# An adaLN block with an S4D convolution and a feed-forward: in block 0, the low part of the first layer's weights by an adding transfer instead of a VectorE subtraction

## The chip, the cores and the metric

The program runs on one core of a Trainium2 chip. The metric is the device time of one execution in microseconds (us). The times given are medians of several runs of the same program.

## The reference

One sequence of 2048 tokens, D = 576 channels, feed-forward width 4608, all in fp32:

```python
mod = (_silu(c) @ w_mod).reshape(c.shape[0], 6, 1, -1)
sa, ca, ga, sb, cb, gb = (mod[:, 0], ..., mod[:, 5])
h = _layernorm(x) * (1 + ca) + sa
x = x + ga * S4D(h)
h = _layernorm(x) * (1 + cb) + sb
x = x + gb * (jnp.maximum(h @ w1, 0) @ w2)
```

`S4D(h)` is a long convolution of each channel with a kernel K that is summed from 128 complex exponentials (`P = jnp.exp((A * dt[:, None])[:, :, None] * pos)`, `K = 2.0 * jnp.einsum("dn,dnl->dl", C, P).real`), plus a skip term.

## The kernel before, in words

**Blocks and chunks.** The tokens are cut into NB = 4 blocks of 512, the hidden channels into NF = 36 chunks of 128. `ffn` (L1242) is one loop over g = 0 to 143, that is block by block and in each block over the 36 chunks. Beside it, in its `step` (L1345), it advances generators that hold all other work: while block 0's feed-forward runs, the rest of the convolution kernel is built and block 1's convolution is done; while block 1's runs, block 2's convolution, and so on.

**Two pieces of each number.** TensorE (PE) multiplies in a format (`fp32r`) that keeps fewer bits than fp32. So every weight and activation is split into a high piece, the rounded value, and a low piece, the remainder, and products of high and low pieces are added up. For the first layer `first(g)` (L1296) issues 14 matmuls of 128x512 into a PSUM tile `hps`, from the weights' pieces `w[:, 0]` (high) and `w[:, 1]` (low) and the block's activations `xh`, `xl`, `xs`. ScalarE (ACT) then takes `hh` = Relu of it (L1314), and VectorE (DVE) the remainder `hl` (L1315). `second(g)` (L1318) issues 14 matmuls from `hh`, `hl` and the second layer's pieces into five accumulators `acc` (L1335).

**The weights' path in block 0.** For each chunk `load_r1` (L1254) brings 320 KB of w1 into a tile `r1` (two buffers), `load_r2` (L1258) 288 KB of w2 into `r2` (two buffers), both on SyncE's (SP's) queue. `hi1` (L1274) is an ACT copy of `r1` into `w1[:, 0]`, which rounds to the high piece. `lo1` (L1279) is a DVE subtraction that writes `r1 − high` to `w1[:, 1]`. `hi2` and `lo2` (L1284, L1290, L1291) do the same for the second layer. The low pieces are then stored to DRAM (`L1d`, `L2d`, L1390, on SP's queue, by way of the list `late`), and blocks 1 to 3 load them from there (`low1`, L1263) instead of making them again; so `lo1` computes only for g < 36. The tiles `w1` and `w2` have three buffers each. A buffer of `r1` comes free for chunk g + 2 when `hi1(g)` and `lo1(g)` have read it.

The loop's order for each g is: `load_r1(g+3)`, `load_r2(g+2)`, the stores in `late`, `first(g)`, `hi2` and `lo2` of g + 1, `hi1` and `lo1` of g + 2, `low1(g+3)`, then `second(g−1)`. Instructions of g < 3 are kept in program order (the profile shows them at the helper's line, L47). For the others a list scheduler decides the order on each engine at build time; at run time each engine and each issuing queue goes through its own list in order and waits where an operand isn't ready.

**The other work of block 0.** `rest` (L436) builds the convolution kernel in 12 heads (h = 0 to 11). For each head POOL's queue loads `W0` (768 KB from `W1d`), `Zr` (96 KB from `Zd`) and `W2r` (1536 KB from `W2d`); DVE turns `W0` into `W1r` by rotations (L464 to L470); PE multiplies `W1r` by `W2r` into `kps` (L498); ACT copies that into `ker` (L508), which is stored as `kd` on SP's queue. A load of `W2r` waits until PE is through with the tile's last use, and everything behind it on POOL's queue waits with it. Then follows block 1's convolution: POOL's queue loads `kt` from `kd` (L1232), PE transforms it into `ps_f` (L829), ACT copies that (L830), DVE does butterflies and complex products with spectra `R`, `Ka`, `Ua` that POOL's queue saves to and loads from DRAM (L816, L820). The inverse goes through `ps_i` (L1036). At the end of block 0 the generator is run out, so that block 1's activations are ready.

The functions and what calls them:

Of the kernel before, what the change touches and what calls it, by code (L numbers as in the profile page):

```python
# [10 lines left out]
F32 = mybir.dt.float32  # L11
F32R = mybir.dt.float32r
I32 = mybir.dt.int32
AF = mybir.ActivationFunctionType
ALU = mybir.AluOpType
# [9 lines left out]
NF = F // P  # L25
# [525 lines left out]
class Body:  # L551
# [194 lines left out]
    def main(self, ctx, kg, hooks):  # L746
# [32 lines left out]
        with ExitStack() as c:  # L779
            self.cps = self.pool(c, "cps0", space=PSUM)  # L780
            self.tps = self.pool(c, "tps", space=PSUM)
            self.cv = self.pool(c, "cv0", side="right")
            self.cvl = self.pool(c, "cvl", side="right")
            self.nps, self.ns = 4, 6
            mods, ffn = self.mod_late(), self.ffn(gens)
            self.vec = Kept(tc, nc.vector)
            for w in self.conv(0):
                if w == "mod":
                    next(mods, None)
                elif w in ("weights", "high", "low"):  # L790
                    next(ffn)
                elif w == "rows":
                    hooks[w]()
                elif w in hooks:
                    for _ in hooks[w]:
                        pass
            self.vec = nc.vector
# [444 lines left out]
    def ffn(self, gens):  # L1242

        nc, I, ff = self.nc, self.I, self.ff
        n = NB * NF
        r1, r2, w1, w2 = {}, {}, {}, {}
# [20 lines left out]
        def vec(g):  # L1267
            return (Kept(self.tc, nc.vector) if g < 3 else nc.vector).tensor_tensor

        def copy(g):  # L1270
            return (Kept(self.tc, nc.scalar) if g < 3 else nc.scalar).activation

        def hi1(g):
            copy(g - 1)(w1[g][:, 0], r1[g], AF.Copy)  # L1274

        def lo1(g):
            w, r = w1[g], r1.pop(g)
            if g < NF:
                vec(g)(w[:, 1], r, w[:, 0], op=ALU.subtract)  # L1279
                late.append((self.L1d[g], w[:, 1].rearrange("p k c -> p (k c)")))  # L1280

        def hi2(g):
# [89 lines left out]
        for f in (hi1, hi2):  # L1372
            f(0)
        hi1(1)
        yield
        lo1(0)
        lo2(0)
        lo1(1)
        yield
        load_r2(1)  # L1380
        load_r1(2)
        prev = None
        for g in range(n + 1):
            if g < n:
                if g + 3 < n:
                    load_r1(g + 3)
                if g + 2 < n:
                    load_r2(g + 2)
                for dst, src in late:
                    nc.sync.dma_start(out=dst, in_=src.bitcast(F32))  # L1390
                late.clear()
                new = (g, *first(g))
                if g + 1 < n:
                    hi2(g + 1)
                    lo2(g + 1)
                if g + 2 < n:
                    hi1(g + 2)
                    lo1(g + 2)
                if g + 3 < n:
                    low1(g + 3)  # L1400
                step(g)
            if prev is not None:
                second(*prev)
                if prev[0] % NF == NF - 1:
                    self.evacuate(prev[0] // NF)
            if g < n:
                prev = new
                step(g)
                if g % NF == NF - 1:
                    for _ in gens[g // NF]:  # L1410
                        pass
                    done[0] = 0.0
# [126 lines left out]
```

## Time and profile before

| | us |
|---|---|
| median of 3 runs | 1362.46 (1361.05 to 1364.14) |
| profiled execution | 1357.89 |
| its span | 1356.1 |

The mean granted clock of TensorE was 0.944 of full speed in the profiled execution. The stages on its time axis are: kernel rows and block 0's convolution until about 222 us, block 0's feed-forward from 222 to about 570 us, of which the heads take 222 to 425 and block 1's convolution 425 to 545, and then blocks 1 to 3 until 1356.

How to read it: PE is TensorE's matmuls, PEld its weight loads, DVE VectorE, ACT ScalarE, POOL GpSimd, SPq the queue of SyncE. A row of a timeline gives start, duration, engine, line, operation and in square brackets the idle time before it and what ended that. A wait row reads "engine, tile and line, waited for what: us in total, times, longest". L12 is line 12 of the kernel; `out<-in` names tiles.

### The profile page before, as it was taken

Reading aid. Unit: us, or ns where it says so; the run is one execution under the profiler, and the core shown is the slowest. Engines: PE = TensorE matmul, PEld = TensorE weight load, DVE = VectorE, ACT = ScalarE, POOL = GpSimd, SP = SyncE. Lnnn points to the kernel's source line nnn. Section 1 sums busy time; section 2 is a strip of 40 time slices with the busy share of each in tenths; the row PEclk is TensorE's granted clock in tenths of the full one; section 3 lists DMA queues with packets and bytes.
Section 4 is the critical chain, followed back from the end, with each engine's and each line's share of the span. In section 5 each row is a group of like instructions: output and inputs, shape, how many; then the busy total and the mean of one; then the engine's idle time right before and its main releaser. Section 6 shows DMA issues by size and latency. Waiting matters only on the chain.

```text
span 1356.1 us, 26019 instructions
## 1 busy us (share of the span) xinstructions
PE 1239.6 (91%) x10720; PEld 986.5 (73%) x10720; DVE 891.6 (66%) x1324; ACT 494.9 (36%) x863; POOL 162.6 (12%) x260
## 2 busy tenths in 40 slices
PE   4566777899989999999999999999999999999997
PEld 2345555677767687777777887887888888888885
DVE  5889988999955899678556986367997222111112
ACT  5678423222122432622234225433322353233231
POOL 0657511000010100020000000100000000000000
PEclk9558887999978999999999999999999999999998
DMA  8557973776897877798778995777996557666651
GB/s 267 221 223 291 328 271 130 282 249 248 320 332 277 296 248 269 239 382 311 250 246 327 363 371 158 269 230 245 370 387 194 176 175 228 201 195 195 201 184 53
DMA packets 120843, 345.85 MB, mean 255 GB/s; under 512 B 23916, under 2 KB 24212, under 8 KB 109972
## 3 DMA queue, kind: packets, MB, share of 16 engines
q1 hardware_dynamic: 103828, 226.96, 49.7%
q0 software_dynamic: 16384, 115.85, 22.8%
q8 instruction: 84, 1.38, 0.4%
q10 hardware_dynamic: 512, 1.38, 0.3%
q14 instruction: 35, 0.29, 0.1%
HBM read 262.73 MB, written 81.40 MB: 254 GB/s over the span
## 4 chain that ended last, share of the span: by engine, by line
PE 73%; DVE 15%; DMA 5%; issue 4%; ACT 1%; POOL 1%; SPq 0%; ACTq 0%; DVEq 0%; POOLq 0%
PE acc L1335 29%; PE hps L1309 29%; PE kps L498 4%; PE ps_f L829 4%; PE kps L71 2%; PE ph L71 2%; PE ps_i L1036 2%; DVE T L464 1%; DVE W1r L466 1%; DVE T L62 1%; DMA Ua<-Ud 1%; DVE Y L1015 1%; DMA r<-in_w_dram 1%; DMA kd<-ker 1%; DVE W L62 1%
## 5 line engine op out<-in xcount | busy, mean ns | idle before, releaser
L1309 PE MATMUL hps<-xh,w 128*128 128x512 f32 x1152 | 391.3, 400 | 0.7 <-ACT xh L47 0.7
L1335 PE MATMUL acc<-w,hh 128*128 128x512 f32 x1152 | 371.8, 403 | 7.0 <-ACT hh L1314 7.0
L1315 DVE SCALAR_TENSOR_TENSOR hl<-hps,hh 128x512 fp32r<-128x512 f32 x144 | 99.0, 687 | 322.9 <-ACT hh L1314 321.9
L1335 PEld LDWEIGHTS acc<-w,hh 128*128 128x128 f32 x1152 | 217.6, 190 | 55.1 <-ACT hh L1314 8.3
L1309 PEld LDWEIGHTS hps<-xh,w 128*128 128x128 f32 x1152 | 217.3, 190 | 48.5 <-ACT xh L47 1.3
L1309 PE MATMUL hps<-xl,w 128*128 128x512 f32 x576 | 230.7, 401 | 0.2
L1335 PE MATMUL acc<-w,hl 128*128 128x512 f32 x576 | 224.4, 402 | 3.9 <-DVE hl L1315 3.9
L1314 ACT ACTIVATE hh<-hps 128x512 fp32r<-128x512 f32 x144 | 85.9, 597 | 304.0 <-PE hps L1309 302.3
L1284 ACT ACTIVATE w<-r 128x576 fp32r<-128x576 f32 x141 | 96.6, 685 | 236.7 <-PE acc L1335 207.9
L1335 PEld LDWEIGHTS acc<-w,hl 128*128 128x128 f32 x576 | 109.1, 190 | 28.2 <-DVE hl L1315 5.0
L1309 PEld LDWEIGHTS hps<-xl,w 128*128 128x128 f32 x576 | 108.7, 189 | 24.5 <-DVE xl L47 0.8
L1274 ACT ACTIVATE w<-r 128x640 fp32r<-128x640 f32 x140 | 102.6, 733 | 40.6 <-DMA r<-in_w_dram 40.6
L1309 PE MATMUL hps<-xs,w 128*128 128x512 f32 x288 | 97.1, 410 | 0.3 <-DVE w L1279 0.3
L498 PEld LDWEIGHTS kps<-W1r,W2r 128*32 128x32 f32 x3456 | 66.9, 146 | 32.0 <-issue 23.6
L498 PE MATMUL kps<-W1r,W2r 128*32 128x48 f32 (+2 forms) x3456 | 75.9, 238 | 9.2 <-issue 8.2
L71 PE MATMUL kps<-W,W 128*32 128x16 f32 x2304 | 45.1, 218 | 42.7 <-POOL W L68 28.7
L71 PEld LDWEIGHTS kps<-W,W 128*32 128x32 f32 x2304 | 40.4, 150 | 55.0 <-POOL W L68 30.7
L1015 DVE TENSOR_TENSOR Y<-Y,T 128x1152 f32<-128x1152 f32 x60 | 79.4, 1349 | 0.0
L830 ACT ACTIVATE Z<-ps_f 128x288 f32<-128x288 f32 x120 | 48.7, 408 | 68.8 <-PE ps_f L829 67.6
L1453 POOL DMA_DIRECT2D out_dram<-x x16 | 8.7, 544 | 469.0 <-DVE x L1445 466.3
L1309 PEld LDWEIGHTS hps<-xs,w 128*128 128x128 f32 x288 | 53.3, 188 | 12.4 <-DVE w L1279 0.7
L1335 PE MATMUL acc<-hl,w 128*128 128x512 f32 x144 | 57.3, 398 | 0.0
(230 smaller groups left out, 1567.3 us busy)
## 6 DMA issues: line engine op xcount, KB each, us to landing
r<-in_w_dram SPq DMA_DIRECT2D x144, 320.0 KB, 3.5
r<-in_w_dram SPq DMA_DIRECT2D x144, 288.0 KB, 3.7
w<-L1d SPq DMA_DIRECT2D x108, 320.0 KB
w<-L2d SPq DMA_DIRECT2D x108, 288.0 KB, 2.6
W2r<-W2d POOLq DMA_DIRECT2D x18, 1536.0 KB, 8.3
W2d<-W SPq DMA_DIRECT2D x12, 1536.0 KB, 8.6
Ua<-Ud POOLq DMA_DIRECT2D x15, 1152.0 KB, 9.4
W<-W1d POOLq DMA_DIRECT2D x18, 768.0 KB, 10.7
```

The costliest lines, as they stand in the source:

```text
L62: self.tc.keep_in_program_order(self.nc.vector.tensor_tensor(out, a, b, op=op))
L71: self.tc.keep_in_program_order(self.nc.tensor.matmul(*args, **kw))
L498: nc.tensor.matmul(ps[32 * dd : 32 * dd + 32, q, :], W2[:, r, :, ch], W1[:, :, r, ch], start=(r == 0), stop=(r == 1),)
L829: nc.tensor.matmul(o, fc[:, n2, c, :], src(n2), start=True, stop=True)
L830: ev = nc.scalar.activation(Z[:, n2, c], ps[:, :PC], AF.Copy)
L1015: v(y, y, T, op=op or ALU.add)
L1274: copy(g - 1)(w1[g][:, 0], r1[g], AF.Copy)
L1284: copy(g)(w[:, 0:D], r2[g], AF.Copy)
L1309: nc.tensor.matmul(ps, a, x, start=(i == 0), stop=(i == 13))
L1314: nc.scalar.activation(hh, ps, AF.Relu)
L1315: nc.vector.scalar_tensor_tensor(hl, ps, 0.0, hh, op0=ALU.max, op1=ALU.subtract)
L1335: nc.tensor.matmul(acc[i], a, x, start=(f == 0 and seen[i] == 1), stop=(f == NF - 1 and seen[i] == (3 if i < 4 else 2)),)
```

## The change

In block 0 (g < 36) the DVE subtraction of `lo1` goes. ACT makes a second copy of `r1`, scaled by −1, into `w1[:, 1]`: the negated high piece. Then a transfer on POOL's (GpSimd's) queue reads `r1` and adds it to what stands in `w1[:, 1]`, which leaves `r1 − high`. The store to `L1d` and the next load into the same `r1` buffer wait for this transfer where they waited for DVE. The second layer's low piece stays a DVE subtraction. There are 36 such copies and 36 such transfers of 320 KB. From here on the changed kernel's lines are numbered five higher (Relu L1319, `acc` L1340, `hi2` L1289, the stores L1395).

```diff
         def hi1(g):
             copy(g - 1)(w1[g][:, 0], r1[g], AF.Copy)
+            if g < NF:
+                copy(g - 1)(w1[g][:, 1], r1[g], AF.Copy, scale=-1.0)
 
         def lo1(g):
             w, r = w1[g], r1.pop(g)
             if g < NF:
-                vec(g)(w[:, 1], r, w[:, 0], op=ALU.subtract)
+                nc.gpsimd.dma_start(
+                    out=w[:, 1].rearrange("p k c -> p (k c)").bitcast(F32),
+                    in_=r.rearrange("p k c -> p (k c)"), accum_op=ALU.add,
+                )
                 late.append((self.L1d[g], w[:, 1].rearrange("p k c -> p (k c)")))
```

The scheduler also moves other instructions. Three places follow. The first is POOL's queue at the start of block 0's feed-forward, where the first heads' data are loaded. Before:

```order
L47 DMA W2r_0_2963<-W2d_0_65 128x3072
L47 DMA W0_1_2965<-W1d_1_78 128x1536
L47 DMA Zr_1_2966<-Zd_1_90 128x192
L47 DMA W0_2_2987<-W1d_2_79 128x1536
L47 DMA Zr_2_2988<-Zd_2_91 128x192
L47 DMA W2r_1_3072<-W2d_1_66 128x3072
```

and with the change, where `w1_2666` and `w1_2989` are chunks 2 and 3:

```order
L47 DMA W2r_0_2965<-W2d_0_65 128x3072
L47 DMA W0_1_2967<-W1d_1_78 128x1536
L47 DMA Zr_1_2968<-Zd_1_90 128x192
L1281 DMA w1_2666<-r1_2938 128x640
L47 DMA W0_2_2990<-W1d_2_79 128x1536
L47 DMA Zr_2_2991<-Zd_2_91 128x192
L1281 DMA w1_2989<-r1_2940 128x640
L47 DMA W2r_1_3076<-W2d_1_66 128x3072
```

Chunk 2's adding transfer stands behind the loads of `W2r_0` and `W0_1`, and two adding transfers stand ahead of `W2r_1`.

The second place is POOL's queue at the end of the heads. Before, the last `W2r`, block 1's `x` and the convolution's `kt` follow one another; with the change, where `w1_4898`, `w1_5102` and `w1_5251` are chunks 19, 20 and 21:

```order
L47 DMA W2r_10_4777<-W2d_10_75 128x3072
L47 DMA W2r_11_4924<-W2d_11_76 128x3072
L1281 DMA w1_4898<-r1_4839 128x640
L47 DMA x2_1_5201<-in_x_dram 128x2304
L1281 DMA w1_5102<-r1_5019 128x640
L1281 DMA w1_5251<-r1_5205 128x640
L1232 DMA kt_5203<-kd_1_0_59 128x16x72
```

`kt` now stands behind three adding transfers. In the same way the loads of `Ua` and `R` of the second half of block 1's convolution stand behind the transfers of chunks 26 to 29.

The third place is ACT's list there. Before, `w1_5230` is chunk 21, and its copy stands ahead of the last four copies of kernel heads:

```order
L1314 ACTIVATE hh_5220<-hps_5191 128x512
L1274 ACTIVATE w1_5230<-r1_5185 128x640
L508 ACTIVATE ker_6_4333<-kps_4916 128x16x6
L508 ACTIVATE ker_6_4333<-kps_4975 128x16x6
L508 ACTIVATE ker_6_4333<-kps_5040 128x16x6
L508 ACTIVATE ker_6_4333<-kps_5108 128x16x6
L1284 ACTIVATE w2_5316<-r2_5187 128x576
L1314 ACTIVATE hh_5312<-hps_5275 128x512
```

With the change, chunk 21 is `w1_5251`:

```order
L1319 ACTIVATE hh_5240<-hps_5211 128x512
L508 ACTIVATE ker_6_4349<-kps_4935 128x16x6
L508 ACTIVATE ker_6_4349<-kps_4994 128x16x6
L508 ACTIVATE ker_6_4349<-kps_5059 128x16x6
L508 ACTIVATE ker_6_4349<-kps_5128 128x16x6
L1289 ACTIVATE w2_5337<-r2_5207 128x576
L1274 ACTIVATE w1_5251<-r1_5205 128x640
L1276 ACTIVATE w1_5251<-r1_5205 128x640
L1319 ACTIVATE hh_5333<-hps_5296 128x512
```

Both copies of chunk 21 (L1274, and L1276 negated) now stand behind the heads' copies and the second layer's copy, just ahead of the next Relu.

## The prediction

> **What bounds the kernel now.** I read the page's first rows, then busy time by stretch, then what TensorE (PE) waits for, then the chain of waits. In the windows the columns are the stretch and its length in us, busy us with instruction counts of PE, PEld, DVE, ACT and POOL, the granted clock, the DMA share and GB/s.
>
> ```profile
> span 1356.1 us, 26019 instructions
> ...
> PE 1239.6 (91%) x10720; PEld 986.5 (73%) x10720; DVE 891.6 (66%) x1324; ACT 494.9 (36%) x863; POOL 162.6 (12%) x260
> ```
> ```profile
> 222.00:253.00 31.00, 26.57 (x115) 19.94 (x118) 29.64 (x34) 11.03 (x18) 4.22 (x8) 0.94 0.71 274
> 253.00:350.00 97.00, 93.86 (x1240) 73.77 (x1232) 97.00 (x101) 22.89 (x40) 7.95 (x15) 0.97 0.73 259
> 350.00:425.00 75.00, 65.95 (x1488) 53.35 (x1488) 45.28 (x62) 14.54 (x31) 8.03 (x14) 0.86 0.87 312
> 425.00:525.00 100.00, 100.00 (x421) 76.59 (x420) 88.71 (x136) 34.63 (x70) 7.56 (x13) 1.00 0.81 287
> 525.00:545.00 20.00, 17.12 (x73) 13.07 (x71) 19.78 (x27) 5.61 (x9) 0.00 (x0) 1.00 0.46 165
> 840.00:1120.00 280.00, 280.00 (x1240) 227.02 (x1239) 172.40 (x242) 109.45 (x196) 12.35 (x22) 1.00 0.73 253
> ```
>
> Block 0's feed-forward runs from 222 to about 570. From 253 to 350, while kernel heads are built, VectorE (DVE) is busy for all of 97.0 us; from 525 to 545 for 19.78 of 20. From 425 to 525 PE is full, and later blocks look like 840 to 1120: PE full, and without this subtraction. So time won or lost in block 0 is carried to the end, and the prize is what PE idles in block 0. Its waits, in us, times and longest, from 222 to 253, 253 to 350, 350 to 425 and 425 to 570:
>
> ```profile
> PE acc L1335 <- ACT hh L1314: 3.8, 2, 2.8
> ...
> PE acc L1335 <- ACT hh L1314: 3.1, 1, 3.1
> ...
> PE kps L498 <- issue: 8.2, 3, 2.8
> PE kps L498 <- ACT ker L508: 0.9, 1, 0.9
> ...
> PE acc L1335 <- DVE hl L1315: 1.7, 1, 1.7
> PE ps_i L1036 <- DVE x L1041: 0.9, 1, 0.9
> PE hps L1309 <- DVE w L1279: 0.3, 1, 0.3
> ```
>
> The 9.1 us at the heads' end (8.2 + 0.9) have no cause in the subtractions. That leaves 3.8 + 3.1 + 2.9 = 9.8 us. The chain (start, duration, what) shows the heads' two paces:
>
> ```profile
> 251.93 3.34 DVE W1r L466 x2
> ...
> 271.29 3.34 DVE W1r L466 x2
> ...
> 280.17 11.73 DMA r<-in_w_dram
> ...
> 307.55 2.95 PE hps L1309 x13
> ...
> 326.11 2.95 PE hps L1309 x13
> ```
>
> While DVE leads, a head (two chunks) takes 271.29 − 251.93 = 19.36 us; once a late w1 load has let PE fall behind, PE leads at 326.11 − 307.55 = 18.56.
>
> **The change part by part.** The groups: VectorE's and ScalarE's (xcount, busy us, mean ns), then DMA from 222 to 570 (queue: packets, MB, share of 16 engines; issues with KB and median us to landing).
>
> ```profile
> L1279 DVE TENSOR_TENSOR w<-r,w 128x640 fp32r<-128x640 f32 x33 | 26.8, 816 | 0.0
> ...
> L1274 ACT ACTIVATE w<-r 128x640 fp32r<-128x640 f32 x35 | 25.7, 733 | 37.2 <-DMA r<-in_w_dram 37.1
> ...
> q1 hardware_dynamic: 21952, 48.44, 39.6%
> ...
> W2r<-W2d POOLq DMA_DIRECT2D x12, 1536.0 KB, 8.3
> r<-in_w_dram SPq DMA_DIRECT2D x37, 320.0 KB, 5.2
> ```
>
> *Removed: the subtraction.* 33 × 0.816 = 26.8 us of DVE in these 348 us. Those under the convolution before 222 lie beside other waits; I price them at nothing, and at no more than their own 3 × 0.82 = 2.5 us if that cover is gone. In the heads, two fewer per head give DVE 19.36 − 1.63 = 17.73 us, under PE's 18.56. PE then sets the pace from the start: 97 us are five heads, 5 × 18.56 = 92.8, a gain of 4.2. I take **−4** (ends 0 and −4.2). What is late next is PE itself.
>
> *Added: the negative copy on ScalarE (ACT).* 36 × 0.733 = 26.4 us. ACT is busy 22.89 of 97, 14.54 of 75 and 34.63 of 100 us, so idle time covers it; behind each copy in ACT's order stands often the next Relu (hh), and one copy ahead of it costs PE 0.73 us where hh is awaited. Three such waits stand above, so 0 to 2.2; I take 0, as the Relu has a chunk's time of slack elsewhere.
>
> *Added: the adding transfer.* No row shows one. Below: a plain 320 KB transfer. At q1's rate, 39.6% of 348 us for 48.44 MB, 0.328 MB take 0.93 us of all 16 engines. Above: two such, 1.86 us, as for a load and a store. At one per 10.5 us (348 / 33) the share rises by 0.09 to 0.18: to 0.82–0.91 in the heads, 0.96–1.05 from 350 to 425, 0.90–0.99 from 425 to 525. Only the middle stretch can overflow, by at most 0.05 × 75 = 4 us, and there the heads' last loads go. I take **+1** (0 to +4), nearer the lower row since the 75 us hold some loads with slack.
>
> The Trainium skill, Collectives: The Full Stack, section "The bandwidth ceiling: the fold count and why AG ≠ RS ≠ AR", says an add in the DMA path reads two sources and ran at 1/1.93 of a copy's rate; by it, an estimate, a transfer takes 0.93 × 1.93 = 1.8 us and the term would be about +3. No run here shows it yet.
>
> *Moved: what stands behind it on POOL's queue, and the loads that it frees.* POOL issues in order. At the start the third chunk's transfer comes behind W2r and W0, and the wait of the next w1 load, formerly for DVE, is for its landing:
>
> ```profile
> 227.43 0.53 POOL L47 DMA_DIRECT2D W2r<-W2d  x1 [9.53 <-PE hps L1309]
> ...
> 230.92 0.33 SPq L1254 DMA_DIRECT2D r<-in_w_dram  x1
> ...
> 240.32 0.74 ACT L1274 ACTIVATE w<-r 128x640 fp32r<-128x640 f32 x1 [7.23 <-DMA r<-in_w_dram]
> ...
> 239.82 0.82 DVE L47 TENSOR_TENSOR w<-r,w 128x64 fp32r<-128x64 f32 x2
> ...
> 240.70 0.33 SPq L1258 DMA_DIRECT2D r<-in_w_dram  x1
> ...
> 250.13 0.68 ACT L1284 ACTIVATE w<-r 128x576 fp32r<-128x576 f32 x1 [8.01 <-DMA r<-in_w_dram]
> ```
>
> W2r at 227.43 + 8.3 lands near 236, the transfer near 238, so the load goes at 238 instead of 230.92; in a less crowded queue it takes 5.2, not 9.4, and lands near 243, some 3 us later than 240.3. The wait of 8.01 ends with an r2 load, issued at 240.70 once DVE had made the second layer's low part at 239.82, which the change leaves there. It sets when PE goes on after 250, so 3 us lost at the first place shorten PE's 2.8 us at the second by as much. I take **0** (−1.5 to +4).
>
> From 350 on, chunk 21's transfer stands ahead of the convolution's kt load, and chunk 29's ahead of the next Ua and R loads:
>
> ```profile
> 404.54 1.18 POOL L1232 DMA_DIRECT2D kt<-kd  x1
> ...
> 423.37 0.68 ACT L1284 ACTIVATE w<-r 128x576 fp32r<-128x576 f32 x1 [0.17 <-PE acc L1335]
> ...
> 434.31 0.65 PE L829 MATMUL ps_f<-kt,fcK 128*128 128x288 f32 x2
> ```
> ```profile
> kt<-kd POOLq DMA_DIRECT2D x2, 576.0 KB, 11.8
> ```
>
> kt was issued 30 us before PE used it. Now hi1(21) and its negative copy follow the ACT copy at 423.37, so POOL gets to kt at about 423.37 + 0.68 + 2 × 0.73 + 0.5 = 426; with the median 11.8 us it lands at 438, 3.5 us late, while with W2r's 8.3 it comes in time. PE's order puts the feed-forward's matmuls behind ps_f, so lateness is paid. I take **+2** (0 to +4).
>
> *The tail.* From 525 to 545 the DVE chain sets the end; two subtractions lie in it, and the 425 to 525 stretch drops some ten:
>
> ```profile
> 525.22 1.36 DVE L1013 TENSOR_TENSOR T<-Ka,Ua 128x1152 f32<-128x1152 f32 x1 [2.03 <-DMA Ua<-Ud]
> ...
> 528.50 0.82 DVE L1279 TENSOR_TENSOR w<-r,w 128x640 fp32r<-128x640 f32 x1
> ...
> 538.19 0.82 DVE L1279 TENSOR_TENSOR w<-r,w 128x640 fp32r<-128x640 f32 x1
> ```
>
> That would win back PE's 2.9 us, but DVE already waits 2.03 us there for Ua, which comes no earlier. I take **−2.5** (−2.9 to +2, if Ua or R come later by as much as that wait).
>
> **Sum.** −4 + 0 + 0 + 1 + 0 + 2 − 2.5 = −3.5 us. The profiled execution took 1357.89 us (1356.1 plus 1.8 around it), so 1354.4 like for like; the median of the runs, 1362.46, lies 4.6 above it, so the median becomes **1359.0**. The likeliest case's own range is 1355 to 1361.
>
> **Rivals.** *Transfers come late and the two r1 buffers decide (slower).* A buffer's turn is the load (5.2), two copies (1.5), the adding transfer, and some 2 us of issue. Two buffers pace a chunk at (8.7 + L)/2 us, which exceeds the present 10.5 once the landing L passes 12.3. An adding transfer behind W2r takes 8.3 + 5.2 = 13.5, and others 5.2: mean 9.4, not enough. If its own part doubles, as two passes would, the mean is (18.7 + 10.4)/2 = 14.6, the pace 11.6, and over the 19 chunks until the heads end (203 us / 10.5) it costs 19 × 1.1 = 21 us, with no gain: about 1383; half as often behind W2r, about 1373. For it speak the wait of 7.23 and the 11.73 us load in the chain, with DMA share 0.73 to 0.87; against it that PE needs only one chunk per 9.3 us and waits for w1 loads now in few places.
>
> *Queues eat the gain (slower).* All upper ends of POOL's moved transfers come together, start +4, kt +4, middle +4, tail 0, against −4 in the heads: +8, with half of it +4: 1366 to 1370. It speaks for this that kt loses nearly all its 30 us of lead, and that the Trainium skill, DMA: Bandwidth & Descriptors, section "Issuing engines are not separate DMA queues", has all issuers share the 16 engines; the shares here, 0.87 for both queues together, agree.
>
> *No change.* DVE was never what PE lacked: in the heads only one wait of 3.1 us is booked to a hh, behind a w1 load, not to DVE. Then the heads give −1 at most, the tail −1, kt +2: 1362.5. Against it stands DVE's 97.0 of 97.
>
> **How the numbers follow.** My sum 0.42; queues eat the gain 0.23; buffers decide 0.17; no change 0.18. About 0.2% (2.7 us) is what a measurement of this kernel can tell. Faster 0.40 (the sum's case less its slow edge), same 0.18, slower 0.42: the two slower cases together outweigh the likeliest one, which gives the time. The range leaves out a better heads stage (below 1353) and the worst of the buffers (above 1379): 1353 to 1379.
>
> **What would show it.** Right: PE's busy share from 253 to 350 rises to the full stretch and the heads end some 4 us earlier; DVE shows idle time there; PE's wait at 242 grows and that at 252 shrinks; L1281 lands within 10 us of its issue. Wrong: PE waits for hh behind w1 loads (ACT w ← DMA r grows past 37.1 us), ps_f waits for kt by more than 4 us, or hps waits for w's low part, which would mean the transfer lands later than a subtraction did. If DMA's share stays under 0.9 from 253 to 350 and the time is still worse, latency in POOL's queue is to blame and not bandwidth.

## The result and the profile after

The change makes the kernel slower: 1384.47 us in the median (1380.08 to 1386.70) beside 1362.70 for the kernel before, a ratio of 1.0156 with a 95% interval of 1.0128 to 1.0184. The prediction said 1359.0. The profiled execution took 1380.08 us, its span 1378.3, which is 22.2 more than the span before.

The first rows of the page of the changed kernel, and its software queue (packets, MB, share of 16 engines):

```profile
span 1378.3 us, 26091 instructions
...
PE 1244.6 (90%) x10720; PEld 991.7 (72%) x10720; DVE 867.2 (63%) x1288; ACT 516.9 (38%) x899; POOL 194.2 (14%) x296
...
q0 software_dynamic: 21568, 127.65, 27.1%
```

PE has the same work (1244.6 us busy beside 1239.6). DVE lost 24.4 us, the subtractions; ACT gained 22.0, the copies. So what changed is what the engines wait for. Busy time by stretch of the changed kernel, in the columns of the prediction:

```profile
222.00:253.00 31.00, 25.87 (x91) 19.56 (x90) 21.87 (x24) 11.56 (x19) 6.06 (x10) 0.79 0.74 256
253.00:350.00 97.00, 90.34 (x1219) 70.84 (x1220) 87.78 (x89) 27.72 (x48) 17.28 (x25) 0.96 0.91 275
350.00:425.00 75.00, 64.13 (x1261) 51.46 (x1261) 44.33 (x49) 19.50 (x38) 12.31 (x19) 0.91 0.92 314
425.00:525.00 100.00, 92.89 (x623) 70.87 (x616) 72.30 (x123) 38.96 (x79) 15.64 (x21) 0.98 0.93 296
```

DVE is no longer full from 253 to 350 (87.78 of 97), as forecast, yet PE is less busy there too (90.34 after 93.86). DMA's share went from 0.73 to 0.91. PE's waits from 222 to 600 in the changed kernel:

```profile
PE hps L1314 <- DMA w<-r: 9.1, 3, 3.7
...
PE kps L498 <- ACT ker L508: 5.3, 2, 4.8
PE ps_i L1036 <- DVE x L1041: 4.2, 2, 2.6
PE acc L1340 <- ACT hh L1319: 4.2, 2, 3.4
```

PE now waits for the adding transfers themselves (9.1 us), one of the prediction's signs of being wrong, and for the copy that empties the one `kps` bank (5.3 after 0.9). No wait of `ps_f` for `kt` stands there. The chain of waits of the changed kernel in the first heads (start, us, what) shows how they hang together:

```profile
235.81 11.06 DMA w<-r
246.93 9.62 DMA r<-in_w_dram
...
266.54 11.97 DMA w<-r
278.56 3.23 DMA r<-in_w_dram
281.95 0.74 ACT w L1274
282.69 0.63 ACT w L1276
283.32 0.32 ACT ker L508
283.68 2.33 PE kps L498 x95
```

These two adding transfers take 11 to 12 us from issue (the median of 19 from 222 to 425 is 7.5). The w1 load into the buffer that one frees follows, ACT's two copies wait for the load, the head's copy `ker` stands behind them on ACT's list, and PE waits for `ker`.

To see where time is lost I take the start of each chunk's Relu on ACT, counted from that of chunk 0, and subtract the same of the kernel before. (Profiled executions differ by up to 4 us from the kernel before in when chunk 0 starts.) Chunk 15 ends most of the heads, 27 stands in block 1's convolution, 36 is the first chunk of block 1. The chunks are from one profiled execution of each kernel, the ratios from all runs; that of e3_plain is the fastest of its ten, 5.4 us under their median, so its chunks may look too good:

| kernel | chunk 15 | 27 | 36 | ratio to before (95%) |
|---|---|---|---|---|
| the change | +13.1 | +14.1 | +21.0 | 1.0156 (1.0128–1.0184) |
| e1_none | +11.6 | +8.2 | +5.6 | 1.0024 (1.0003–1.0045) |
| e2_neg | −1.3 | 0.0 | −0.1 | 1.0001 (0.9982–1.0020) |
| e3_plain | +5.0 | +3.4 | +4.7 | 1.0049 (1.0027–1.0072) |
| e4_r1x3 | +14.8 | +16.6 | +16.8 | 1.0110 (1.0066–1.0155) |
| e8_late20 | −0.6 | +2.5 | +6.8 | 1.0041 (1.0025–1.0057) |
| e9_none_held | −5.0 | −4.7 | −7.3 | 0.9925 (0.9901–0.9950) |
| e13_plain_twice | +16.0 | +21.4 | +29.8 | 1.0180 (1.0163–1.0198) |

So the change loses 13 us in the heads, 1 to chunk 27, and 7 at the tail, where 6.5 were to be won.

### The profile page after: what moved, and what is told of

The parts are those of the page before. It is cut to its first block, busy times and chain, and to the rows that moved or that the text cites. A ratio compares the mean times of both kernels' runs of the same rounds, so it can differ in the third digit from the quotient of the medians.

```text
span 1378.3 us, 26091 instructions
## 1 busy us (share of the span) xinstructions
PE 1244.6 (90%) x10720; PEld 991.7 (72%) x10720; DVE 867.2 (63%) x1288; ACT 516.9 (38%) x899; POOL 194.2 (14%) x296
## 4 chain that ended last, share of the span: by engine, by line
PE 74%; DMA 10%; DVE 7%; issue 6%; ACT 2%; POOL 1%; SPq 0%; POOLq 0%; ACTq 0%; DVEq 0%
PE acc L1340 29%; PE hps L1314 29%; DMA w<-r 4%; PE kps L498 4%; DMA r<-in_w_dram 4%; PE ps_f L829 4%; PE kps L71 2%; PE ph L71 2%; PE ps_i L1036 2%; DVE T L62 1%; DVE k L62 1%; PE ps_t L1131 1%; POOL W L68 1%; DMA L2d<-w 1%; DVE W L62 1%
## 5 line engine op out<-in xcount | busy, mean ns | idle before, releaser
L1340 PE MATMUL acc<-w,hh 128*128 128x512 f32 x1152 | 370.3, 403 | 4.2 <-ACT hh L1319 4.2
L1340 PEld LDWEIGHTS acc<-w,hh 128*128 128x128 f32 x1152 | 218.0, 190 | 52.1 <-ACT hh L1319 5.0
L1314 PEld LDWEIGHTS hps<-xh,w 128*128 128x128 f32 x1152 | 220.3, 192 | 48.5 <-ACT xh L47 1.3
L1314 PE MATMUL hps<-xl,w 128*128 128x512 f32 x576 | 234.0, 407 | 0.1
L1340 PE MATMUL acc<-w,hl 128*128 128x512 f32 x576 | 225.8, 401 | 0.9 <-DVE hl L1320 0.9
L1289 ACT ACTIVATE w<-r 128x576 fp32r<-128x576 f32 x141 | 96.6, 685 | 260.0 <-PE acc L1340 180.8
L1319 ACT ACTIVATE hh<-hps 128x512 fp32r<-128x512 f32 x144 | 85.8, 596 | 287.0 <-PE hps L1314 284.6
L1340 PEld LDWEIGHTS acc<-w,hl 128*128 128x128 f32 x576 | 109.2, 190 | 24.4 <-DVE hl L1320 1.5
L1274 ACT ACTIVATE w<-r 128x640 fp32r<-128x640 f32 x140 | 102.7, 733 | 50.3 <-DMA r<-in_w_dram 50.1
L1340 PE MATMUL acc<-hl,w 128*128 128x512 f32 x144 | 57.2, 397 | 0.0
```

Of the source, the lines that this page charges most:

```text
L1289: copy(g)(w[:, 0:D], r2[g], AF.Copy)
L1314: nc.tensor.matmul(ps, a, x, start=(i == 0), stop=(i == 13))
L1319: nc.scalar.activation(hh, ps, AF.Relu)
L1340: nc.tensor.matmul(acc[i], a, x, start=(f == 0 and seen[i] == 1), stop=(f == NF - 1 and seen[i] == (3 if i < 4 else 2)),)
```

## The experiments

**Is the gain there at all, and do ACT's copies cost?** e1_none drops the subtraction and puts nothing in its place (the negated copy is left as the low piece); e2_neg makes the copies and keeps the subtraction.

```diff
e1_none, against the change:
-                nc.gpsimd.dma_start(out=w[:, 1]..., in_=r..., accum_op=ALU.add)
e2_neg, against the change:
-                nc.gpsimd.dma_start(out=w[:, 1]..., in_=r..., accum_op=ALU.add)
+                vec(g)(w[:, 1], r, w[:, 0], op=ALU.subtract)
```

> Leaves out the low part of the first layer's weights in block 0 (no subtraction and no adding transfer; the negated copy stands in its place), so the output is not the reference's. It measures what taking the subtraction from VectorE is worth with nothing put in its place. The prediction's terms: heads -4, tail -2.5, so 1356 (1354 to 1360). Rival, that the subtraction never set PE's pace: 1362 +- 2. Both theories of the loss (transfers late in POOL's queue, or DMA bandwidth) say it must be below 1363; if ACT's extra copies are the cost it stays above 1370.

> The negated copy on ACT is made, but VectorE still subtracts (it overwrites the negated copy), no adding transfer: the copy's cost alone. Transfers at fault: 1362 +- 3. ACT's copies at fault: 1370 or more.

The copies cost nothing that can be told: 1.0001 (0.9982 to 1.0020). But without any transfer the kernel was not faster either: 1.0024. Its chunk 15 is 11.6 us late, so something else in the heads took the gain and more. PE's waits of e1_none, from 222 to 330 and from 330 to 425, and a piece of its ACT timeline:

```profile
PE kps L498 <- ACT ker L508: 8.8, 3, 7.4
...
PE kps L498 <- ACT ker L508: 6.9, 3, 3.8
```
```profile
337.59 0.68 ACT L1285 ACTIVATE w<-r 128x576 fp32r<-128x576 f32 x1 [7.02 <-DMA r<-in_w_dram]
338.18 0.72 ACT L1274 ACTIVATE w<-r 128x640 fp32r<-128x640 f32 x1
338.81 0.72 ACT L1276 ACTIVATE w<-r 128x640 fp32r<-128x640 f32 x1
339.44 0.40 ACT L508 ACTIVATE ker<-kps 128x288 f32<-128x288 f32 x1
```

ACT waits 7.02 us for a w2 load, and `ker`, which PE waits for, stands behind it. In ACT's list before, the two head copies that follow `hh` of chunk 5 stand ahead of `hi1(8)`; in the change and in e1_none, `hi1(8)` and its negated copy stand ahead of both. With no late VectorE instruction to hold r1, the scheduler put weight copies further ahead. SP's list moved as well. In the kernel before, loads of w1 and w2 take turns; in e1_none the r1 loads of chunks 4 to 7 stand ahead of the w2 load of chunk 4, and they wait for ACT's copies. So ACT waits for late w2 loads, from 222 to 425 before, in e1_none and in e9_none_held below:

```profile
ACT w L1284 <- DMA r<-in_w_dram: 8.0, 1, 8.0
```
```profile
ACT w L1285 <- DMA r<-in_w_dram: 40.1, 10, 7.0
```
```profile
ACT w L1286 <- DMA r<-in_w_dram: 8.2, 2, 4.4
```

**The same without that order.** e9_none_held leaves VectorE 8 of the 640 columns, which brings `ker` back ahead of `hi1(8)`, and on SP's list w1 and w2 loads take turns again.

```diff
e9_none_held, against e2_neg:
-                vec(g)(w[:, 1], r, w[:, 0], op=ALU.subtract)
+                vec(g)(w[:, 1, 0, :8], r[:, 0, :8], w[:, 0, 0, :8], op=ALU.subtract)
```

> No adding transfer, and of the subtraction only 8 of 640 columns remain on VectorE (the rest of the low piece is left out, the negated copy stands there; output not the reference's). The small instruction holds each r1 buffer until DVE's list reaches it, so that the order of ACT's list is nearly that of before again: the head copies (ker) no longer stand behind the weight copies of a chunk further ahead. If that order ate the gain, PE's waits for ker (15.7 us in e1_none) fall below 4 and the time is 1354 to 1357. If weight loads pace the heads in any order, it stays at 1360 to 1363.

0.9925 (0.9901 to 0.9950), 1351.8 us, below the range expected. ACT's timeline of e9_none_held and PE's wait for `ker` there, 330 to 425:

```profile
279.64 0.43 ACT L508 ACTIVATE ker<-kps 128x288 f32<-128x288 f32 x1 [3.19 <-PE kps L498]
279.96 0.73 ACT L1274 ACTIVATE w<-r 128x640 fp32r<-128x640 f32 x1
280.58 0.73 ACT L1276 ACTIVATE w<-r 128x640 fp32r<-128x640 f32 x1
```
```profile
PE kps L498 <- ACT ker L508: 0.2, 1, 0.2
```

Now `ker` waits only for PE, and goes first; PE is busy for all of the 97 us from 253 to 350. The heads gain 5.0 us and the tail 2.6, what the prediction had put at 4 and 2.5. One per cent, the distance from e1_none to e9_none_held, is a matter of the lists' order, or of the small instruction itself, the only other difference. Whether ACT's list or SP's carries it no run separates, as both came back together.

**What does the add cost?** In e3_plain the transfer is a plain copy; every engine's list is the same, instruction by instruction, as in the change.

```diff
e3_plain, against the change:
-                    in_=r.rearrange("p k c -> p (k c)"), accum_op=ALU.add,
+                    in_=r.rearrange("p k c -> p (k c)"),
e13_plain_twice, against e3_plain, with self.Sx unused DRAM tiles:
+                nc.gpsimd.dma_start(out=self.Sx[g], in_=r.rearrange("p k c -> p (k c)"))
```

> The same transfer at the same place of POOL's queue, but a plain copy instead of an add, so the low part is the whole weight and the output is not the reference's. If an add costs the 16 DMA engines two passes, their time on POOL's queue falls by about 0.9 us for each transfer (32 us in all). If bandwidth is the cause the loss of 22 us halves: 1371 to 1375. If waiting behind W2r and W0 in the queue is the cause, most stays: 1377 to 1383.

> As e3_plain, with a second plain transfer of the same 320 KB behind it into an unused DRAM tile (output not the reference's): the DMA time of two copies, about 1.6 us for each chunk against 1.8 of an add, and r1 held until both have landed. If an add costs what two copies cost, the loss is nearly that of the change: ratio 1.012 to 1.018. If the add has a delay of its own, it stays near 1.007.

1.0049 for the plain transfer, under both ranges expected, 1.0156 for the add, 1.0180 for two plain transfers. So of the change's 1.56%, 1.07% (14.6 us) is the add alone. From issue to landing, 222 to 425, an add takes 8.0 us on average and a plain copy 6.8; SP's wait for them (`SPq L1254 <- DMA w<-r`) is 98.0 and 88.2 us. The software queue's row on the pages of the kernel before, of e3_plain and of e13_plain_twice:

```profile
q0 software_dynamic: 16384, 115.85, 22.8%
```
```profile
q0 software_dynamic: 19264, 127.65, 24.9%
```
```profile
q0 software_dynamic: 22144, 139.45, 26.8%
```

Share times span, less the 309.2 us of before: 29.0 us for e3_plain's 36 copies, 0.81 each (24.9% of its 1358.3), and 64.3 for the change's 36 adds, 1.79 each. An add takes 2.2 times a copy's engine time, in 144 packets for 80. The Trainium skill, Collectives: The Full Stack, section "The bandwidth ceiling: the fold count and why AG ≠ RS ≠ AR", has an adding transfer read two sources at 1/1.93 of a copy's rate, measured there on collectives; 2.2 here is near it.

**Is it the crowded engines?** W2r is loaded for every second head only; two heads then share one W2r, so the convolution kernel isn't the reference's.

```diff
e5, e6, e7, against before, e1_none and the change:
-                if i + 1 < len(hs):
+                if i + 1 < len(hs) and (len(hs) < 12 or i % 2):
                     W2 = load2(hs[i + 1])
```

> Control: the kernel before, which loads W2r only for every second head and uses it twice, so the kernel heads, and the output, are not the reference's; 6 x 1.57 MB less to move between 222 and 425 us. VectorE's pace as the limit: 1359 +- 3, no gain, since DVE has the same work. Weight loads delayed by W2r as the limit: 1352 or less.

> No subtraction, no adding transfer (low piece left out) and W2r loaded for every second head only. If the missing subtraction brought nothing because weight loads stuck behind W2r set the heads' pace, it now shows: 3 to 8 us below the control. If the order on ACT's list (head copies behind weight copies) is the cause, it stays at the control or above it.

> The changed kernel with W2r loaded for every second head only (output not the reference's). If crowded DMA engines make the loss in the heads, the 12 us there shrink to 4 or less and the distance to the control is 8 to 12 us (the tail's part). If it is the order of ACT's list or the r1 buffers, the distance stays near 20 us.

Ratios to the kernel before: 0.9922 (0.9901 to 0.9944), 0.9954 (0.9937 to 0.9972) and 1.0114 (1.0078 to 1.0150). The kernel before does gain 11 us, but the distance of the change to its control did not shrink (1.6%, now 1.9%), and chunk 15 is still 15.6 us late. DMA's shares in e7 are 0.79 from 253 to 350 and 0.80 from 350 to 425, a landing takes 6.0 us on average, and PE waits 15.9 us for `ker` from 222 to 425. So room on the 16 engines doesn't undo the loss, and the mean landing alone doesn't set it either: it is shorter here than in e3_plain. The missing gain of e1_none stays too (e6 0.3% above e5).

**Is it the two r1 buffers, or SP's list?** To make room for the third buffer, e4_r1x3 and e12_r1x3_hi also put `o4` into the tile of `kt` and give block 1 one `W0` buffer fewer. In e12_r1x3_hi blocks 1 to 3 use a wrong low piece.

```diff
e4_r1x3, against the change:
-            r1[g] = ff.tile([P, 5, P], F32, tag="r1", bufs=2, name="r1")
+            r1[g] = ff.tile([P, 5, P], F32, tag="r1", bufs=3, name="r1")
e12_r1x3_hi, against e4_r1x3:
-                late.append((self.L1d[g], w[:, 1].rearrange("p k c -> p (k c)")))
+                late.append((self.L1d[g], w[:, 0].rearrange("p k c -> p (k c)")))
```

> The changed kernel with a third r1 buffer (its space comes from sharing a tile with kt and from one W0 buffer fewer in block 1). If the two r1 buffers held by late transfers set the heads' pace, the 12 us lost between 240 and 360 us shrink to under 4 and the time is 1370 to 1375. If bandwidth is the cause, it stays at 1382 or above. The loss of 8 to 10 us between 512 and 547 us stays in both.

> As e4_r1x3 (three r1 buffers), and the L1d stores take the high piece in place of the low one (so blocks 1 to 3 use a wrong low piece), so that no store on SP's queue waits for the adding transfer; only r1 loads do, one chunk later than before. If SP's list standing on the transfer, with the w2 loads behind it, makes the heads' loss, the 13.8 us of e4_r1x3 at chunk 14 shrink to 7 or less. If the transfer's lateness reaches PE by w's low part itself, PE's wait for w <- r grows and the loss stays above 10.

With three buffers the tail's loss is gone (16.6 at chunk 27, 16.8 at 36; the change has 14.1 and 21.0), and the ratio is 1.0110 (1.0066 to 1.0155), an interval that overlaps the change's. The heads' loss is not gone (14.8). The time expected, 1370 to 1375, nearly came (1375.4), but by luck: the heads' loss was to shrink and the tail's to stay. Why the heads' loss stays, the wait of SP's queue from 222 to 425 shows; first the change, then e4_r1x3:

```profile
SPq L1254 <- DMA w<-r: 98.0, 15, 12.7
```
```profile
SPq L1395 <- DMA w<-r: 107.6, 17, 14.5
```

The wait only moved from the r1 load (L1254) to the store of the low piece (L1395), which stands ahead of the next loads on the same list. e12_r1x3_hi takes that store's wait for the transfer away too, and got slower: 1.0236 (1.0214 to 1.0258), chunk 15 late by 31.2 us. Its SP and ACT waits, 222 to 425:

```profile
SPq L1395 <- ACT w L1274: 71.5, 11, 12.0
SPq L1254 <- DMA w<-r: 56.1, 12, 6.5
```
```profile
ACT w L1289 <- DMA r<-in_w_dram: 92.0, 14, 14.0
```

SP stands less on the transfer, but the store now stands on ACT's copy (71.5 us), so SP's list wasn't freed; ACT waits 92.0 us for w2 loads (54.0 in the change) and PE 22.1 us for `ker`. In both kernels with three buffers SP's list has the r1 load of chunk 9 ahead of the w2 load of chunk 6; in the change the last ahead of it is that of chunk 7, and in the kernel before that of chunk 6. So the edit brought an order of its own, and neither cut settles what carries the loss in the heads; why e12_r1x3_hi is worse than e4_r1x3 stays open.

**Holding r1 as in e9, with the adding transfer.**

```diff
e10_after_held, against the change:
+                z = ff.tile([P, 8], F32, tag="z1", bufs=2, name="z1")
+                vec(g)(z, r[:, 0, :8], r[:, 0, :8], op=ALU.subtract)
```

> The changed kernel plus a VectorE instruction on 8 columns of r1 (into a scratch tile) for each chunk, which holds r1 as in e9_none_held and lets the head copies go ahead on ACT's list. If the order made the heads' loss, at most 5 of the 12 us stay and the time is 1370 to 1377; the tail's 8 us stay. If the adding transfer's own lateness made it, PE waits for w <- r or for hh instead and the time stays at 1380 or above.

1.0345 (1.0318 to 1.0372): much worse. The head copies do stand ahead of the weight copies again, yet PE waits 18.4 us for `ker` from 222 to 425: ACT waits 81.3 us for weight loads there, and `ker` still stands behind the copies that follow them. So the order of ACT's list alone doesn't keep `ker` early; the loads must be early too. By the lists, the weight copies come later, and with them the adding transfer, its landing and the next load; no run separates these. Holding r1 helped only in e9_none_held, where only 8 columns of the low piece are made.

**Heads and tail apart.** The change for some chunks only, VectorE for the others.

```diff
e8_late20; e11_heads has g < 20 in both places:
+            if 20 <= g < NF:
                 copy(g - 1)(w1[g][:, 1], r1[g], AF.Copy, scale=-1.0)
...
+                if 20 <= g < NF:
                     nc.gpsimd.dma_start(out=w[:, 1]..., in_=r..., accum_op=ALU.add)
+                else:
+                    vec(g)(w[:, 1], r, w[:, 0], op=ALU.subtract)
```

> Adding transfers only from chunk 20 on, VectorE subtracts for chunks 0 to 19. If the losses of the heads and of the tail are separate, the tail's 8 to 10 us stay: 1367 to 1370. If the tail loses only since the heads ended late: 1363 or less.

> Adding transfers for chunks 0 to 19 only, VectorE subtracts from chunk 20 on. With e8_late20 (+5 us, all of it after 500 us) as the other half: if the halves add up, +17 us, 1374 to 1378, all of it before 425 us.

1.0041 and 1.0115 (1.0049 to 1.0181): together the change's 1.0156, though only within that wide interval; by the medians they lose 5.2 and 21.4 us, together more than the change's 21.8. e8_late20 loses 2.5 us by chunk 27 and 4.3 more by 36, between its two cases. e11_heads loses all of its time by chunk 15 (27.7 us in its profiled execution, twice the change's; its runs spread from 1366 to 1386), so the heads' loss varies much, between executions too.

**VectorE freed by GpSimd instead.** No transfer, everything computed:

```diff
e15_gpsimd, against before; e14_gpsimd_held has the two lines of e10_after_held besides:
-                vec(g)(w[:, 1], r, w[:, 0], op=ALU.subtract)
+                nc.gpsimd.tensor_tensor(w[:, 1], r, w[:, 0], op=ALU.subtract)
```

> The kernel before with the first layer's subtraction on GpSimd (by L68's rows, 1.016 us for 384 columns, about 1.7 us for 640) and the small VectorE instruction that holds r1 as in e9_none_held; no adding transfer, no negated copy. Everything is computed. If the gain of e9_none_held (about 9 us) is to be had whenever VectorE is freed, no transfer is added and ACT's order kept: 1352 to 1357. If POOL's queue, where loads of W2r now stand behind subtractions, is the hindrance: 1360 or more.

> As e14_gpsimd_held without the small VectorE instruction: the head copies stand again behind weight copies of a chunk further ahead on ACT's list. If the order eats the gain as in e1_none, 5 us or more above e14_gpsimd_held, 1360 to 1365.

1.0438 (1.0400 to 1.0476) and 1.0160 (1.0128 to 1.0191). e14_gpsimd_held came out on the side of its second case, 60 us above the 1360 given there; e15_gpsimd, expected above it, is 38 us below. The groups of e14_gpsimd_held, GpSimd's and VectorE's, from 222 to 620:

```profile
L1279 POOL TENSOR_TENSOR w<-r,w 128x640 fp32r<-128x640 f32 x34 | 72.8, 2142 | 166.5 <-ACT w L1274 154.1 <-DMA L1d<-w 10.8 <-ACT w L47 1.5
```
```profile
L1293 DVE TENSOR_TENSOR w<-r,w 128x512 fp32r<-128x512 f32 x33 | 29.6, 896 | 0.0
```

The subtraction takes 2142 ns on average on GpSimd, its list waits 154.1 us for `hi1`, with the loads of W2r behind it, and as in e10 the holding instruction made it worse (PE waits 22.6 us for `ker` from 222 to 425). Which of these costs the time no run separates.

No kernel that computes everything beat the kernel before.

## Why the prediction was wrong

- **VectorE's relief in the heads (−4) and at the tail (−2.5)** was sized rightly, 5.0 and 2.6 in e9_none_held, but it holds only with the lists as they were. The step that failed is "What is late next is PE itself". With the lists that the change brings, `ker` stands behind weight copies, these wait for loads, and PE waits for `ker`; in e1_none the whole gain is gone by the order alone. In place of −4 the heads lost 13.1 us. The prediction looked at ACT's new list near chunk 21 only, not in the heads, and not at SP's; it had set PE's wait of 0.9 us for `ker` aside as having no cause in the subtractions.
- **The adding transfer (+1, 0 to +4)** is the step that failed most. Its engine time was taken "nearer the lower row", 0.93; it measured 1.79, close to the upper bound of 1.86. The estimate by two reads, 1.8, was the better guide. And the step priced it by DMA's share alone. The shares rose to 0.91 and 0.93, as computed, and in the middle stretch, the only one priced, to 0.92, below the computed 0.96; but in e7 the loss stayed at 0.79 and 0.80. The transfer's landing is now a link between r1's load and the next, on lists that go in order; e3_plain and the change differ in nothing but the kind of transfer, and by 14.6 us. The sign that was to tell latency from bandwidth, a share under 0.9 from 253 to 350, decides nothing at 0.91.
- **ACT's copies (0)**: right, e2_neg.
- **The start (0, −1.5 to +4)**: inside its range; chunk 4 is 1.9 us late. As forecast, most of what the first place loses the second wins back, but it is 9.1 us at chunk 2 where 3 were forecast.
- **kt (+2)**: the size fits, the mechanism doesn't. From chunk 15 to 27 the change loses 1.0 us, but PE does not wait for `kt`: it is issued at 440.4 and lands 7.7 us later, and PE, busy until then, comes to `ps_f` at 448.5, 14 us later than before. So the agreement is luck.
- **The tail (−2.5, to +2)** went to +6.9 from chunk 27 to 36. VectorE's wait for `Ua` after 470 grew only from 2.0 to 4.4 us. With the third r1 buffer the loss is gone in e4_r1x3, though `Ua` is waited for there for 3.2 us; so the r1 buffers, not `Ua` and `R`, are the likely cause, as far as one profiled execution of a kernel with other lists shows it.
- **The rivals.** "Transfers come late and the two r1 buffers decide" came nearest in time (1373 to 1383), and fits the tail. In the heads the third buffer won nothing, and its point of decision, a mean landing over 12.3 us, wasn't reached: the mean is 8.0 and the median 7.5 from 222 to 425, and only 3 of 19 take 11 us or more. "No change", since DVE was never what PE lacked, is refuted by e9_none_held.
- **The range** left out 1384 as "the worst of the buffers".

What stays open is which link in the heads would have to be cut to free the change from its loss. Cutting r1's (e4) and the store's (e12) moved the wait on; a kernel with the change's transfer and all lists of the kernel before was not made. That the loss in the heads goes the way of the chain above is read from the traces; by experiment it is shown only that, with all lists the same, an add in place of a copy adds 14.6 us.

## What to carry to other kernels

An instruction that is removed also removes a hold: before counting its time as won, read from the new order what moves ahead on every in-order list, and what a short, urgent copy now stands behind. An adding transfer cost about two copies here, and it turned a dependence of under 1 us on an engine into one of 4 to 15 us on a queue; one more buffer on one side of it did not make it pay. When a cost is bounded by two rows, the nature of the operation (here two reads) says which bound it is nearer to.

## What was not expected of the hardware

- Beside GpSimd's subtraction a few instructions are slowed a great deal and most not at all. VectorE's 128x512 subtraction of the second layer took 896 ns on average in e14_gpsimd_held and 681 before; but five of 33 took 2.0 to 2.4 us, each while a GpSimd subtraction ran, and the median is 678. GpSimd's own took 2142 ns on average for 640 columns; the median of those from 222 to 570, 1.6 us, is about what L68's rows (1016 ns for 384) give by an estimate, 1.7 us, and single ones took up to 5 us.
- While two layers' weights and W2r are loaded, halving W2r's loads alone gave 0.8% (e5), at a mean DMA share of only 0.73 from 253 to 350 in the kernel before; in e5 it is 0.66, and PE is busy for all of the 97 us (93.86 before). Which load comes sooner to effect was not tested.
